# Batch 0's k loaded in fp32, its last tiles normalised in halves, v spread by VectorE: an attention and MLP kernel on one core

## The chip, the cores and the metric

The kernel runs on one core of a Trainium2 chip. The metric is the device time of one launch in microseconds. Kernels are compared by the median of several runs; three runs of the kernel before took 302.98, 303.24 and 303.75 us.

The core has a matrix engine (TensorE, PE in the profile; its weight loads are PEld), VectorE (DVE), ScalarE (ACT), GpSimd (POOL) and a queue engine (SyncE, SP). Matrix products land in PSUM, everything else lies in SBUF. DMAs are issued by SP, ScalarE or POOL and carried out by 16 DMA engines.

## The reference

Inputs are q, k and v of shape (8, 8, 576, 64): batch, heads, positions, features. The attention is linear, with ReLU features weighted by a cosine and a sine of the position, and its output goes through an MLP whose nonlinearity is h * cos(h):

```python
r = np.maximum(x, 0.0)                                   # phi, for q and for k
phi = np.concatenate([r * c, r * s], axis=-1)            # c, s: cos, sin of pi/2 * pos / 576
kv = np.einsum('bhsf,bhsd->bhfd', k_p, v)
z = np.sum(k_p, axis=2)
num = np.einsum('bhsf,bhfd->bhsd', q_p, kv)
den = np.einsum('bhsf,bhf->bhs', q_p, z)[..., None] + 1e-06
x = (num / den)                                          # to (4608, 512): token, head * 64 + feature
h = x @ w_in                                             # 512 -> 2048
out = (h * np.cos(h)) @ w_out                            # 2048 -> 512
```

## The kernel before

**Tiling.** The 576 positions of a batch lie as 96 partitions times six runs: partition p holds positions 6p to 6p + 5, and "run i" is the i-th of the six. The MLP takes the 4608 tokens in nine chunks of 512, so chunks and batches don't line up. A batch's attention output is made in five tiles of 128 tokens (the last adds 64 new ones).

**The attention of one batch.** `load` brings q, k, v from memory through POOL's queue and casts them to fp16 on the way (k16, v16, q16, two buffers each). `scaled` makes ReLU times cosine and ReLU times sine of one run, two instructions of 96x512 for all heads (96x256 for four heads, as batch 0's k is taken), on VectorE, with a few of batch 0 on ScalarE. `q_turn` turns a run of scaled q so that features lie on partitions (X): by PE and a copy out of PSUM for batches 0 and 1, by a DMA transpose on SP's queue from batch 2 on. `spread_v` copies two heads of v into rows of 66 (vz), of which the last two hold ones, so that one product gives kv and z; batch 0 does without. `kv_head` does the six matmuls of a head; ScalarE copies the result to kvz. `num_tile` makes numerator and denominator of a tile on PE (NP), and VectorE adds 1e-6 (dn), inverts (rd) and multiplies (x: the "normalise"). `x_turn` turns x to XT, the MLP's input: by PE (XP) and a copy for batches 0 and 1, by a DMA transpose from batch 2 on.

**The MLP of one chunk.** `m1_group(c, j)`, j from 0 to 15, makes 128 of the 2048 columns of h with four matmuls, then ScalarE makes the cosine (co) and VectorE the product (g). The PSUM tile of group j is free again when its g is done; there are four such tiles, two for even and two for odd j. Chunk 0's groups are done in two halves of 256 tokens, 32 half groups. `m2_part(c, m, part)` adds four of the 16 matmuls of 128 output rows; after the fourth, ScalarE copies the tile out (ost) and SP stores it.

**The order** is written out by hand: engines run their instructions in program order, and `plan` says which attention step follows which MLP step. `at(c, s, f, ...)` puts a step behind MLP step s of chunk c, in the order of the `at` calls. For chunk 0, slots 0 to 31 are its half groups (`HS` = 16), and slots z + 0 to z + 15 (z = 32) its output parts. For chunks 1 to 8, slots 0 to 15 are groups and 16 to 31 (`M2S` = 16) output parts. `plan_tiles` puts tile t of batch c + 1 at M2S + 2t, so the last one at M2S + 8; `plan_ahead` puts the scalings, turnings and copies of batch c + 2 into the same stretch.

**Buffers that matter here.** x has three buffers (`opool`): tile 3's normalise waits until tile 0's x has been turned, tile 4's until tile 1's has. co has three buffers too. The pool "att" in PSUM has two tiles, which QT, KV, NP and XP take in turn.

**The start** (lines 375 to 424): the constants CS (cosines and sines) and ID (identity for turning) through SP; k in two halves of four heads, q, v and the weights through POOL; `warm(n)`, n matmuls on zeros, which keep PE busy until the first data is there; then k's and q's scalings, the first turnings, kv, and tiles 0 to 2 of batch 0.

Of the kernel before, what the change touches and what calls it, by code (L numbers as in the profile page):

```python
# [10 lines left out]
AF = mybir.ActivationFunctionType  # L11
ALU = mybir.AluOpType
F32 = mybir.dt.float32
# [4 lines left out]
def kernel(  # L18
# [9 lines left out]
    nc = tc.nc  # L28
    B, H, S, D = q.shape
    Dm, Dff = moe_w_in.shape  # L30
    P = 128
    F = 2 * D
    R = 6
    PR = S // R
# [6 lines left out]
    RUN = R * D  # L41
# [9 lines left out]
    cs_dr = nc.inline_tensor(cs_np, name="cs_const")  # L51
# [10 lines left out]
    CS = cpool.tile([PR, 2, R], F32, name="CS")  # L62
# [13 lines left out]
    def tiles_for(b):  # L76
        st[b] = dict(
            k16=lpool.tile([PR, H * RUN], F16, name="k16", tag="k16"),
            v16=lpool.tile([PR, H * RUN + D], F16, name="v16", tag="v16"),
            q16=lpool.tile([PR, H * RUN], F16, name="q16", tag="q16"),  # L80
        )

    def load(b, which, h0=0, h1=H, i0=0, i1=R):
        src = dict(k=k, v=v, q=q)[which]
        dst = st[b][which + "16"][:, 0:H * RUN]
        dst = dst.rearrange("p (h r) -> p h r", h=H)
        nc.gpsimd.dma_start(  # L87
            out=dst[:, h0:h1, i0 * D:i1 * D],
            in_=src[b].rearrange("h (p i) d -> p h (i d)", i=R)[:, h0:h1, i0 * D:i1 * D],
        )  # L90
# [9 lines left out]
    def scaled(b, which, i, h0=0, h1=H):  # L100
        s = st[b]
        if which + "p" not in s:
            s[which + "p"] = apool.tile([PR, R, H * F], F16, name=which + "p",
                                        tag=which + "p", bufs=1)
        dst = s[which + "p"][:, i].rearrange("p (h t d) -> p h t d", t=2, d=D)
        src = s[which + "16"][:, 0:H * RUN].rearrange("p (h i d) -> p h i d", i=R, d=D)
        for t in range(2):
            if b == 0 and (which == "k" and h0 == 4 and t == 1 or which == "q" and i == 4):
                nc.scalar.activation(
                    out=dst[:, h0:h1, t, :], in_=src[:, h0:h1, i, :], func=AF.Relu,  # L110
                    scale=CS[:, t, i:i + 1],
                )
                continue
            nc.vector.tensor_scalar(  # L114
                out=dst[:, h0:h1, t, :], in0=src[:, h0:h1, i, :],
                scalar1=0.0, scalar2=CS[:, t, i:i + 1],
                op0=ALU.max, op1=ALU.mult,
            )

    def q_turn(b, i, tag="m1"):  # L120
        s = st[b]
        if i == 0:
            s["X"] = apool.tile([P, H, S], F16, name="X", tag="X")
        if b >= 2:
            nc.sync.dma_start_transpose(
                out=s["X"][:, :, i * PR:(i + 1) * PR], in_=s["qp"][:, i],
            )
            return
        if b == 1:
            if i % 2 == 0:  # L130
                s["QT"] = psA.tile([P, 2, H, P], F16, name="QT", tag="att")
            QT = s["QT"][:, i % 2]
        elif i >= 4:
            QT = psA.tile([P, 2, H, P], F16, name="QT", tag="att")[:, 0]
        else:
            QT = psM.tile([P, H, P], F16, name="QT", tag=tag)
        for h in range(H):
            nc.tensor.matmul(  # L138
                QT[:, h, 0:PR], lhsT=s["qp"][:, i, h * F:(h + 1) * F], rhs=ID[0:PR, 0:PR],
                is_transpose=True,  # L140
            )
        if b == 1 and i % 2 == 0:
            return
        i0 = i - (b == 1)
        dst = s["X"][:, :, i0 * PR:(i + 1) * PR]
        if b == 0 and i == 2:
            nc.vector.tensor_copy(out=dst, in_=QT[:, :, 0:PR])
        elif b == 1 and i > 1:
            nc.vector.tensor_copy(
                out=dst.rearrange("p h (a c) -> p a h c", a=2),  # L150
                in_=s["QT"][:, :, :, 0:PR],
            )
        elif b == 1:
            nc.scalar.activation(
                out=dst.rearrange("p h (a c) -> p a h c", a=2),
                in_=s["QT"][:, :, :, 0:PR], func=AF.Copy,
            )
        else:
            nc.scalar.activation(out=dst, in_=QT[:, :, 0:PR], func=AF.Copy)

    def spread_v(b, h):
        s = st[b]
        if h == 0:
            s["vz"] = apool.tile([PR, H, R, VS], F16, name="vz", tag="vz", bufs=1)
            nc.gpsimd.memset(s["vz"][:, :, :, D:VS], 1.0)  # L165
        src = s["v16"][:, 0:H * RUN].rearrange("p (h i d) -> p h i d", i=R, d=D)
        nc.scalar.activation(  # L167
            out=s["vz"][:, h:h + 2, :, 0:D], in_=src[:, h:h + 2], func=AF.Copy,
        )

    def kv_head(b, h):
        s = st[b]
# [24 lines left out]
                func=AF.Copy,  # L197
            )

    def num_tile(b, t):  # L200
        s = st[b]
        c0 = min(t * P, S - P)
        NP = psA.tile([P, 2, 512], F32, name="NP", tag="att")
        for h in range(H):
            o = (h % 4) * (D + 1)
            nc.tensor.matmul(  # L206
                NP[:, h // 4, o:o + D + 1],
                lhsT=s["X"][:, h, c0:c0 + P], rhs=s["kvz"][:, h],
                start=True, stop=True,
            )  # L210
        np4 = NP[:, :, 0:4 * (D + 1)].rearrange("p a (h e) -> p a h e", e=D + 1)
        dn = opool.tile([P, 2, 4, 1], F32, name="dn", tag="dn")
        nc.vector.tensor_scalar(  # L213
            out=dn, in0=np4[:, :, :, D:D + 1], scalar1=1e-6, scalar2=None, op0=ALU.add,
        )
        rd = opool.tile([P, 2, 4, 1], F32, name="rd", tag="rd")
        nc.vector.reciprocal(out=rd, in_=dn)  # L217
        x = opool.tile([P, Dm], F16, name="x", tag="x")
        nc.vector.tensor_tensor(  # L219
            out=x.rearrange("p (a h e) -> p a h e", a=2, e=D),  # L220
            in0=np4[:, :, :, 0:D], in1=rd.broadcast_to((P, 2, 4, D)), op=ALU.mult,
        )
        s["x", t] = x

    def x_turn(b, t):
        x = st[b]["x", t]
# [65 lines left out]
    def at(c, s, f, *args):  # L292
        plan.setdefault((c, s), []).append((f, args))
# [8 lines left out]

    def plan_stage0():
        at(0, 1, q_turn, 0, 4)
        at(0, 2, scaled, 0, "q", 5)
        at(0, 3, x_turn, 0, 2)
        at(0, 5, q_turn, 0, 5)
        at(0, 8, num_tile, 0, 3)
        at(0, 14, x_turn, 0, 3)
        at(0, HS + 6, num_tile, 0, 4)  # L310
        at(0, HS + 12, x_turn, 0, 4)
        z = 2 * HS
        for i in range(R):
            at(0, z + i // 2, scaled, 1, "k", i)
            at(0, z + 3 + i // 2, scaled, 1, "q", i)
        for n in range(4):
            at(0, z + 1 + n, spread_v, 1, 2 * n)
        for h in range(4):
            at(0, z + 4, kv_head, 1, h)
        for i in range(2):  # L320
            at(0, z + 5, q_turn, 1, i)
        for h in range(4, H):
            at(0, z + 5, kv_head, 1, h)
        for i in range(2, R):
            at(0, z + 5 + i // 2, q_turn, 1, i)
        for n, f, t in ((7, num_tile, 0), (8, num_tile, 1), (9, x_turn, 0),
                        (10, num_tile, 2), (10, x_turn, 1), (12, num_tile, 3),
                        (12, x_turn, 2), (13, x_turn, 3), (14, num_tile, 4),
                        (15, x_turn, 4)):
            at(0, z + n, f, 1, t)  # L330
        for i, n in enumerate((9, 10, 10, 11, 12, 13)):
            at(0, z + n, scaled, 2, "k", i)
        for n in range(4):
            at(0, z + 12 + n, spread_v, 2, 2 * n)
        for i, n in enumerate((-1, 1, 2, 4, 6, 8)):
            at(0 if n < 0 else 1, z + 15 if n < 0 else n, scaled, 2, "q", i)
            at(0 if n < 0 else 1, z + 15 if n < 0 else n, q_turn, 2, i)
        at(1, 9, loads, 3)
        for h in range(H):
            at(1, 5 + h // 4, kv_head, 2, h)  # L340
# [32 lines left out]
            f(*args)  # L373

    with tc.manual_schedule():
        nc.sync.dma_start(out=CS, in_=cs_dr.ap())
        nc.sync.dma_start(out=ID, in_=id_dr.ap())
        nc.vector.memset(WU, 0.0)
        nc.vector.memset(PIH, math.pi / 2.0)  # L379
        nc.scalar.activation(out=WS, in_=PIH, func=AF.Sin)  # L380
        tiles_for(0)
        load(0, "k", 0, 4)
        load(0, "k", 4, 8)
        load(0, "q", 0, H, 0, 4)
        load(0, "v", 0, 4)
        load(0, "v", 4, 8)
# [13 lines left out]
        def warm(n):  # L400
            for _ in range(n):
                nc.tensor.matmul(W, lhsT=WU[:, 0:P], rhs=WU, start=True, stop=True)  # L402

        warm(29)
        for h0 in (0, 4):
            for i in range(R):
                scaled(0, "k", i, h0, h0 + 4)
# [64 lines left out]
```

## Time and profile before

| what | value |
|---|---|
| median of three runs | 303.24 us |
| the profiled execution: its own time, its span | 303.31 us, 301.50 us |
| mean granted TensorE clock | 0.997 |
| start to 12.16 us | PE busy 9.82, DVE 6.27, ACT 4.52, POOL 8.41 |
| chunk 0's groups, 19.07 to 37.46 (18.39) | PE 16.66, DVE 15.08, ACT 16.29 |
| chunk 0's output and batch 1, 37.46 to 58.66 (21.20) | PE 20.30, DVE 17.46, ACT 12.02 |
| chunk 1, 58.66 to 89.12 (30.46) | PE 30.46, DVE 21.59, ACT 17.57 |
| chunk 4, 150.23 to 180.68 (30.45) | PE 30.45, DVE 21.30, ACT 17.09 |

The rows by stretch give each engine's busy time within it. A busy PE is not PE at its peak, since matmuls are pipelined and their ends are modelled. A line of a timeline reads: start, length (of all instructions merged in the line), engine, line of the kernel, operation, output and inputs, sizes, count, and in brackets the engine's idle time just before with what ended it. The costliest rows on the page (busy us, mean ns of one, idle before):

```profile
L272 PE MATMUL M<-w_out_sb,g 128*128 128x512 f16 x576 | 132.3, 379 | 0.1
L262 DVE TENSOR_TENSOR g<-M,co 128x512 f16<-128x512 f32 (+1 forms) x160 | 99.2, 635 | 51.3 <-ACT co L259 51.0
L253 PE MATMUL M<-XT,w_in_sb 128*128 128x512 f16 (+1 forms) x640 | 129.5, 358 | 1.7 <-DVE g L262 0.9
L167 ACT ACTIVATE vz<-v 96x768 f16<-96x768 f16 x28 | 21.9, 830 | 0.0
```

### The profile page before, as it was taken

How to read it: one execution, taken by the hardware profiler on the slowest of the kernel's cores; microseconds unless marked ns; L12 is line 12 of the kernel's file. 1: busy time of each engine (PE TensorE's matmuls, PEld its weight loads, DVE VectorE, ACT ScalarE, POOL GpSimd, SP SyncE). 2: the span in 40 equal slices, each digit the busy share in tenths (PEclk: the TensorE clock that was granted, in tenths of full speed). 3: DMA queues.
4: the chain of work that ended last, by engine and by line, in shares of the span. 5: the costliest groups of instructions: out<-in, count | busy, mean ns of one | idle time of the engine just before them, and what ended most of it. 6: DMA issues, size and time to landing. Idle time of an engine off the chain costs nothing.

```text
span 301.5 us, 5553 instructions
## 1 busy us (share of the span) xinstructions
PE 291.5 (97%) x2091; PEld 152.7 (51%) x2091; DVE 192.4 (64%) x482; ACT 164.5 (55%) x265; POOL 28.1 (9%) x47
## 2 busy tenths in 40 slices
PE   8898999899999999999999999999999999999993
PEld 3667766454544554455445544554455444444441
DVE  2777996788579675967396839786765257007600
ACT  2578953877157715771577158715772178127521
POOL 8432103003000200021001100000000000000000
PEclk9999999999999999999999999999999999999998
DMA  7999999997996299439973997326612510121022
GB/s 102 196 205 206 204 205 204 238 188 112 190 182 154 38 187 218 112 94 172 216 145 82 166 200 162 88 61 125 154 37 52 130 41 0 35 74 33 0 70 70
DMA packets 73483, 38.81 MB, mean 129 GB/s; under 512 B 46320, under 2 KB 68848, under 8 KB 73456
## 3 DMA queue, kind: packets, MB, share of 16 engines
q0 software_dynamic: 23856, 18.35, 40.4%
q1 hardware_dynamic: 49600, 20.10, 32.4%
q8 instruction: 16, 0.26, 0.4%
q14 instruction: 11, 0.09, 0.1%
HBM read 36.74 MB, written 9.44 MB: 153 GB/s over the span
## 4 chain that ended last, share of the span: by engine, by line
PE 88%; DVE 5%; DMA 3%; ACT 2%; issue 1%; POOL 0%; ACTq 0%; POOLq 0%
PE M L272 41%; PE M L253 38%; PE KV L180 4%; PE NP L206 3%; DMA q<-in_q_dram 3%; DVE g L262 2%; DVE x L219 1%; ACT co L259 1%; PE QT L138 1%; PE KV L190 1%; PE XP L238 1%; DVE qp L114 1%; POOL k L87 0%; DVE rd L217 0%; ACT XT L246 0%
## 5 line engine op out<-in xcount | busy, mean ns | idle before, releaser
L272 PE MATMUL M<-w_out_sb,g 128*128 128x512 f16 x576 | 132.3, 379 | 0.1
L262 DVE TENSOR_TENSOR g<-M,co 128x512 f16<-128x512 f32 (+1 forms) x160 | 99.2, 635 | 51.3 <-ACT co L259 51.0
L253 PE MATMUL M<-XT,w_in_sb 128*128 128x512 f16 (+1 forms) x640 | 129.5, 358 | 1.7 <-DVE g L262 0.9
L259 ACT ACTIVATE co<-M,PIH 128x512 f32<-128x512 f32 (+1 forms) x160 | 102.2, 645 | 28.4 <-PE M L253 26.2
L253 PEld LDWEIGHTS <-w_in_sb 128*128 128x128 f16 x640 | 61.3, 98 | 61.1 <-issue 2.6
L272 PEld LDWEIGHTS <-g 128*128 128x128 f16 x576 | 53.8, 98 | 58.7 <-issue 0.3
L279 ACT ACTIVATE ost<-M 128x512 f32<-128x512 f32 x36 | 21.5, 598 | 89.0 <-PE M L272 81.3
L219 DVE TENSOR_TENSOR x<-NP,rd 128x512 f16<-128x512 f32 x40 | 27.7, 691 | 18.8 <-DMA XT<-x 17.7
L114 DVE TENSOR_SCALAR kp<-k,CS 96x512 f16<-96x512 f16 (+1 forms) x102 | 28.6, 348 | 4.8 <-DMA k<-in_k_dram 4.8
L114 DVE TENSOR_SCALAR qp<-q,CS 96x512 f16<-96x512 f16 x94 | 28.1, 346 | 0.2 <-DMA q<-in_q_dram 0.2
L167 ACT ACTIVATE vz<-v 96x768 f16<-96x768 f16 x28 | 21.9, 830 | 0.0
L206 PEld LDWEIGHTS <-X 128*128 128x128 f16 x320 | 15.5, 98 | 8.3 <-issue 0.2
L206 PE MATMUL NP<-kvz,X 128*128 128x65 f16 x320 | 17.0, 194 | 0.0
L165 POOL MEMSET vz<- 96x96 f16 x7 | 1.3, 188 | 146.0 <-PE KV L180 118.1
L180 PEld LDWEIGHTS <-kp 96*128 96x128 f16 x336 | 12.5, 98 | 3.1
L180 PE MATMUL KV<-vz,kp 96*128 96x65 f16 x336 | 13.0, 193 | 0.0
L213 DVE TENSOR_SCALAR dn<-NP 128x8 f32<-128x8 f32 x40 | 6.5, 162 | 9.3 <-PE NP L206 8.7
L402 PE MATMUL W<-WU 128*128 128x512 f16 x35 | 10.7, 466 | 1.2 <-DVE PIH L379 1.2
L217 DVE RECIPROCAL rd<-dn 128x8 f32<-128x8 f32 x40 | 8.1, 203 | 1.4
L195 ACT ACTIVATE kvz<-KV 128x260 f16<-128x260 f32 x16 | 6.2, 387 | 4.4 <-PE KV L180 2.0
L87 POOL DMA_DIRECT2D q<-in_q_dram x9 | 7.0, 775 | 7.3 <-DVE qp L114 3.7
L87 POOL DMA_DIRECT2D k<-in_k_dram x9 | 6.9, 769 | 3.5 <-DVE g L262 2.1
(27 smaller groups left out, 58.6 us busy)
## 6 DMA issues: line engine op xcount, KB each, us to landing
out_dram<-ost SPq DMA_DIRECT2D x24, 192.0 KB, 2.4
k<-in_k_dram POOLq DMA_DIRECT2D x7, 576.0 KB, 9.5
v<-in_v_dram POOLq DMA_DIRECT2D x7, 576.0 KB, 12.9
q<-in_q_dram POOLq DMA_DIRECT2D x7, 576.0 KB, 7.4
out_dram<-ost SPq DMA_DIRECT2D x24, 128.0 KB, 2.4
w_in_sb<-in_moe_w_in_dram POOLq DMA_DIRECT2D x4, 512.0 KB, 13.9
w_out_sb<-in_moe_w_out_dram POOLq DMA_DIRECT2D x4, 512.0 KB, 19.4
out_dram<-ost SPq DMA_DIRECT2D x24, 64.0 KB, 2.0
```

The costliest lines, as they stand in the source:

```text
L87: nc.gpsimd.dma_start(out=dst[:, h0:h1, i0 * D:i1 * D], in_=src[b].rearrange("h (p i) d -> p h (i d)", i=R)[:, h0:h1, i0 * D:i1 * D],)
L114: nc.vector.tensor_scalar(out=dst[:, h0:h1, t, :], in0=src[:, h0:h1, i, :], scalar1=0.0, scalar2=CS[:, t, i:i + 1], op0=ALU.max, op1=ALU.mult,
L167: nc.scalar.activation(out=s["vz"][:, h:h + 2, :, 0:D], in_=src[:, h:h + 2], func=AF.Copy,)
L180: nc.tensor.matmul(s["KV"][:, h, 0:n], lhsT=s["kp"][:, i, h * F:(h + 1) * F], rhs=s["vz"][:, h, i, 0:n], start=(i == 0), stop=(i == R - 1),)
L206: nc.tensor.matmul(NP[:, h // 4, o:o + D + 1], lhsT=s["X"][:, h, c0:c0 + P], rhs=s["kvz"][:, h], start=True, stop=True,)
L219: nc.vector.tensor_tensor(out=x.rearrange("p (a h e) -> p a h e", a=2, e=D), in0=np4[:, :, :, 0:D], in1=rd.broadcast_to((P, 2, 4, D)), op= ...
L253: nc.tensor.matmul(M1[:, n0:n1], lhsT=w_in_sb[:, i, j * P:(j + 1) * P], rhs=XT[:, i, c * CH + n0:c * CH + n1], start=(i == 0), stop=(i == ...
L259: nc.scalar.activation(out=co[:, n0:n1], in_=M1[:, n0:n1], func=AF.Sin, bias=PIH, scale=1.0,)
L262: nc.vector.tensor_tensor(out=st["g", c][:, j, n0:n1], in0=M1[:, n0:n1], in1=co[:, n0:n1], op=ALU.mult,)
L272: nc.tensor.matmul(M2, lhsT=st["g", c][:, j, m * P:(m + 1) * P], rhs=w_out_sb[:, j], start=(j == 0), stop=(j == NJT - 1),)
L279: nc.scalar.activation(out=ost, in_=M2, func=AF.Copy)
L402: nc.tensor.matmul(W, lhsT=WU[:, 0:P], rhs=WU, start=True, stop=True)
```

## The change

Five things are altered. The two halves of batch 0's k go through SP's queue, uncast, into an fp32 tile k32, which `scaled` then reads; CS and ID go through ScalarE's queue. X of batch 0's run 2 is copied by ScalarE instead of VectorE. `spread_v` stays on ScalarE for batch 1 alone and goes to VectorE for batches 2 to 7. `num_tile` can leave out the normalise, which `normalise` then does by halves of the heads; batch 0's tiles 3 and 4 use this, one half behind each of the next two half groups. And some steps move: batch 0's last q turning from slot 5 to 6, its tile 3 from 8 to 9, the turning of tile 4 from HS + 12 to HS + 11; of batch 1 the turnings of tiles 2 and 3 by one slot, that of tile 4 from z + 15 to behind group 2 of chunk 1. Fillers at the start are 26 instead of 29.

```diff
-        src = s[which + "16"][:, 0:H * RUN].rearrange("p (h i d) -> p h i d", i=R, d=D)
+        src = s["k32" if b == 0 and which == "k" else which + "16"]
+        src = src[:, 0:H * RUN].rearrange("p (h i d) -> p h i d", i=R, d=D)
...
-        if b == 0 and i == 2:
-            nc.vector.tensor_copy(out=dst, in_=QT[:, :, 0:PR])
-        elif b == 1 and i > 1:
+        if b == 1 and i > 1:
...
-        nc.scalar.activation(
-            out=s["vz"][:, h:h + 2, :, 0:D], in_=src[:, h:h + 2], func=AF.Copy,
-        )
+        dst = s["vz"][:, h:h + 2, :, 0:D]
+        if b == 1:
+            nc.scalar.activation(out=dst, in_=src[:, h:h + 2], func=AF.Copy)
+        else:
+            nc.vector.tensor_copy(out=dst, in_=src[:, h:h + 2])
...
-    def num_tile(b, t):
+    def num_tile(b, t, whole=True):
...
+        s["x", t] = x
+        s["norm", t] = (x.rearrange("p (a h e) -> p a h e", a=2, e=D), np4, rd)
+        if whole:
+            normalise(b, t, 0, 2)
+
+    def normalise(b, t, a0, a1):
+        x4, np4, rd = st[b]["norm", t]
         nc.vector.tensor_tensor(
-            out=x.rearrange("p (a h e) -> p a h e", a=2, e=D),
-            in0=np4[:, :, :, 0:D], in1=rd.broadcast_to((P, 2, 4, D)), op=ALU.mult,
-        )
-        s["x", t] = x
+            out=x4[:, a0:a1], in0=np4[:, a0:a1, :, 0:D],
+            in1=rd[:, a0:a1].broadcast_to((P, a1 - a0, 4, D)), op=ALU.mult,
+        )
...
-        at(0, 5, q_turn, 0, 5)
-        at(0, 8, num_tile, 0, 3)
-        at(0, 14, x_turn, 0, 3)
-        at(0, HS + 6, num_tile, 0, 4)
-        at(0, HS + 12, x_turn, 0, 4)
+        at(0, 6, q_turn, 0, 5)
+        for t, n in ((3, 9), (4, HS + 6)):
+            at(0, n, num_tile, 0, t, False)
+            at(0, n + 1, normalise, 0, t, 0, 1)
+            at(0, n + 2, normalise, 0, t, 1, 2)
+            at(0, n + 5, x_turn, 0, t)
...
-                        (12, x_turn, 2), (13, x_turn, 3), (14, num_tile, 4),
-                        (15, x_turn, 4)):
+                        (13, x_turn, 2), (14, x_turn, 3), (14, num_tile, 4)):
             at(0, z + n, f, 1, t)
+        at(1, 2, x_turn, 1, 4)
...
-        nc.sync.dma_start(out=CS, in_=cs_dr.ap())
-        nc.sync.dma_start(out=ID, in_=id_dr.ap())
+        tiles_for(0)
+        st[0]["k32"] = gpool.tile([PR, H * RUN], F32, name="k32", tag="g")
+        k32_v = st[0]["k32"].rearrange("p (h r) -> p h r", h=H)
+        k0_v = k[0].rearrange("h (p i) d -> p h (i d)", i=R)
+        for h0 in (0, 4):
+            nc.sync.dma_start(out=k32_v[:, h0:h0 + 4], in_=k0_v[:, h0:h0 + 4])
+        nc.scalar.dma_start(out=CS, in_=cs_dr.ap())
+        nc.scalar.dma_start(out=ID, in_=id_dr.ap())
...
-        tiles_for(0)
-        load(0, "k", 0, 4)
-        load(0, "k", 4, 8)
...
-        warm(29)
+        warm(26)
```

## The prediction

> **What bounds the kernel now.** I read the page first, then the chain of waits, and then TensorE's and VectorE's timelines wherever that chain leaves TensorE.
>
> ```profile
> PE 291.5 (97%) x2091; PEld 152.7 (51%) x2091; DVE 192.4 (64%) x482; ACT 164.5 (55%) x265; POOL 28.1 (9%) x47
> PE 88%; DVE 5%; DMA 3%; ACT 2%; issue 1%; POOL 0%; ACTq 0%; POOLq 0%
> ```
>
> TensorE (PE) ends the program. From 58.83 us the chain names nothing but PE until the last output copy, so a saving counts only where PE stands still, and work added elsewhere costs only where it makes PE stand still. PE stands still in three places. The start (timeline of VectorE, 0 to 13):
>
> ```profile
> 6.00 4.23 DVE L114 TENSOR_SCALAR kp<-k,CS 96x256 f16<-96x256 f16 x18 [4.84 <-DMA k<-in_k_dram]
> 10.40 2.61 DVE L114 TENSOR_SCALAR qp<-q,CS 96x512 f16<-96x512 f16 x8 [0.17 <-DMA q<-in_q_dram]
> ```
>
> VectorE scales k from 6.00 to 10.23 and q from 10.40, when q has landed (the chain: q issued at 2.78, 7.60 long). PE's first turning follows at 11.07. Two limits nearly coincide: k's scaling, 0.17 us ahead, and q's landing.
>
> Chunk 0's first product, 19 to 38 (PE's timeline):
>
> ```profile
> 22.72 0.51 PE L138 MATMUL QT<-ID,qp 96*128 96x96 f16 x8 [0.30 <-DVE qp L114]
> ...
> 27.05 1.03 PE L253 MATMUL M<-XT,w_in_sb 128*128 128x256 f16 x8 [0.50 <-DVE g L262]
> ...
> 29.13 3.22 PE L253 MATMUL M<-XT,w_in_sb 128*128 128x256 f16 x28 [0.39 <-ACT XT L246]
> ...
> 34.74 1.03 PE L253 MATMUL M<-XT,w_in_sb 128*128 128x256 f16 x8 [0.39 <-DVE g L262]
> ```
>
> The brackets give PE's idle time and its releaser: q's run 5 scaled late, g delayed by a normalise, tile 3's turning late, g again.
>
> The end of batch 1 (PE, 53 to 60):
>
> ```profile
> 54.12 1.03 PE L272 MATMUL M<-w_out_sb,g 128*128 128x512 f16 x4
> 55.69 0.40 PE L238 MATMUL XP<-ID,x 128*128 128x128 f16 x4 [0.54 <-ACT vz L167]
> ...
> 57.05 1.02 PE L272 MATMUL M<-w_out_sb,g 128*128 128x512 f16 x4
> 58.43 0.40 PE L238 MATMUL XP<-ID,x 128*128 128x128 f16 x4 [0.36 <-DVE x L219]
> ```
>
> The first wait is put down to a ScalarE copy; but that turning reads x of tile 3, which VectorE finished at 55.63 (54.94 + 0.69), so the normalise is the true releaser.
>
> Last, where PE does not stop yet (VectorE, entering chunks 4 and 5, whose first matmuls start at 150.23 and 180.68):
>
> ```profile
> 149.36 0.69 DVE L219 TENSOR_TENSOR x<-NP,rd 128x512 f16<-128x512 f32 x1 [2.21 <-DMA XT<-x]
> ...
> 152.59 1.28 DVE L262 TENSOR_TENSOR g<-M,co 128x512 f16<-128x512 f32 x2
> ```
>
> ```profile
> 180.12 0.69 DVE L219 TENSOR_TENSOR x<-NP,rd 128x512 f16<-128x512 f32 x1 [1.49 <-DMA XT<-x]
> ...
> 183.36 1.28 DVE L262 TENSOR_TENSOR g<-M,co 128x512 f16<-128x512 f32 x2
> ```
>
> The last tile's normalise waits for a transpose by DMA, then ten scalings follow without a gap, then the first g of the next chunk.
>
> **The change, part by part.** Prices are sums on the profiled execution: 303.31 us, span 301.50 and 1.81 around it, 0.07 above the median of 303.24.
>
> *k of batch 0.* Two POOL issues (1.31 to 2.79) go; SP issues the halves from 0.75. No row shows so large a load there. On SP's queue CS (4.5 KB) landed 1.5 us after issue, a 192 KB store 2.3 us after in a stretch without loads (213 to 230), but 5.6 us in one with loads (103 to 118). Half of k reads 590 KB; the loads land 205 GB/s in fp16, 410 read, so 1.44 us. The quiet price is 1.5 + 1.44 = 2.9, landing at 3.7; POOL's own k took 4.69, which from 0.75 is 5.4. k now starts before any other load, so I take 4.5. VectorE's scaling reads fp32 instead of fp16. Its bounds for 256 elements: 0.195 apart on fp16 (seven from 8.79 lasted 1.44, the last 0.27 of it), 0.34 apart for g of 256 fp32 values from PSUM (four in 1.44 at 26.58). I take 0.263, near the middle, since the source is as wide as the second's and lies where the first's does. 18 x 0.263 = 4.73, and 0.6 more: the first twelve before ran 0.05 slower than the last six, while POOL was issuing DMAs. So k is scaled at 4.5 + 5.3 = 9.8. q lands earlier too, since the same bytes start about 0.9 sooner: about 9.6. q's scaling starts near 9.95 instead of 10.40: **-0.45**. Ends: -1.0 (q's landing then decides) and +1.6 (5.4 + 18 x 0.34 + 0.6 = 12.1 against 10.4).
>
> [...]
>
> CS and ID move to ScalarE's queue, two issues (0.35 and 0.42) ahead of a table load whose first user comes at 7.45: nothing, with 4 us of cover. v has to be there for PE at 12.16 and 13.5, less the gain; it stands behind 1.5 us less on POOL. Three fewer fillers, 0.22 each, end before the first turning: nothing.
>
> *X of run 2 by ScalarE.* VectorE loses 0.56 at 15.38 just ahead of tile 0's normalise, which then waits for PE's numerator (15.77): **-0.05**. ScalarE has 0.7 idle there.
>
> *Chunk 0's first product.* q's run 5 is turned one slot later; a group of 0.437 (4 x 0.109) fills PE's gap (22.26 to 22.72). g then runs to the new slot 9: numerator at 24.35, g 9 at 25.40, dn and rd 0.43, halves of 0.34 with a g of 0.34 between. Halving only spreads the delay: the second half ends at 27.6, the turning starts at 27.7 instead of 27.92, its copy at 28.1, and the second half of the chunk at 28.75 instead of 29.13. For tile 4, g is no longer late at 34.74, but x is ready 6.0 us into this half and the turning, moved a slot up, stands waiting for it from 5.5: the stall moves and stays. **-0.38** in all; ends 0 and -1.2 (both g stalls gone as well).
>
> *End of batch 1.* Tile 3's turning moves behind one more output part and tile 4's into chunk 1. From 53.64 PE then has 0.26 + 0.86 + 0.22 + 0.86 + 0.22 + 0.26 + 0.86 = 3.54 without a wait (x of tile 3 is ready at 55.63, its turning due at 55.84), so chunk 1 starts at 57.18 instead of 58.66; tile 4's 0.22 comes back later: **-1.26**. VectorE gets batch 2's four copies here and its first g is 0.5 late, under the 0.84 that PE had spare.
>
> *v of batches 3 to 7 by VectorE.* Four copies in each second product leave ScalarE, which PE does not wait for, so nothing is won. No row shows such a copy. Scalings of 256 and 512 elements from SBUF start 0.195 and 0.263 apart, so 768 gives 0.33; the other end is 0.56, a 768 copy out of PSUM. I take 0.33, as both sides lie in SBUF. They stand in slots 8 to 14, all behind the last tile's normalise, which waits for the DMA; so 1.32 us comes ahead of the next chunk's first g. The matmul group 4 needs that g's PSUM buffer, 4 x 0.863 = 3.45 after the chunk starts. Spare time before: chunk 4, 153.68 - 153.28 = 0.40, so PE stops 0.92; chunk 5, 184.13 - 184.05 = 0.08, so 1.24; chunk 2, VectorE was free at 90.63, so g ends at 92.64 against 92.57: 0.07; chunk 3 (free at 121.12) just fits; chunk 6, where VectorE was idle some 4 us, hides it. **+2.23**. With 0.56 it is 5.8.
>
> Sum: -0.45 - 0.05 - 0.38 - 1.26 + 2.23 = +0.09, so 303.31 becomes **303.4**.
>
> **Rivals.** (A) is the sum. (B) *The copies cost nothing*: the last normalise starts early enough. It started 1.89 us before chunk 3 but only 0.87 and 0.56 before 4 and 5, as loads in the same stretch held up the transposes (7.7 us to land against 2.4 without). From 1.8 us before on, the stalls vanish: 303.4 - 2.2 = 301.2. For it: the spread among three alike stretches. Against: nothing in the change moves those loads. (C) *k gains nothing*: q's packets, on POOL's queue from 2.6 on, share the engines with k's, as stores took 5.6 instead of 2.3. With k at 6.5 the start gets 1.5 worse than now: 305.3 at the worst, 304.4 with k at 5.5. Against: k is ahead of all loads. [...] (D) *Slower*: the copies run at the PSUM row's 0.56, and PE stops 5.8 us at chunks 2 to 5: 307.0; from about 0.39 a copy the total passes 0.3%. For it: the scattered rows of 64 they write; against: kp's scaling writes such rows too at 0.195 for 256.
>
> **How the numbers follow.** A 0.43, B 0.25, C 0.16, D 0.16. About 0.3% (0.9 us) is what this kernel's times can tell from no change. Faster: B and 0.08 of A's lower edge, 0.33. Same: 0.28 of A and 0.04 of C, 0.32. Slower: 0.07 of A, 0.12 of C, D: 0.35. A alone spans 302.2 to 304.6 (its two uncertain terms, start and stalls, about 0.8 each); the range reaches to B's 301.2 and to C's 305.3, leaving out most of D.
>
> **What would show it.** Right: k's scaling from about 4.5, 0.26 apart; chunk 1 starting 1.5 us nearer to the tile-3 numerator; group 4 of chunks 4 and 5 waiting about 1 us for g. Wrong: no wait of PE for g after 60 us (B), q's scaling after 10.4 (C), copies of 0.5 (D).

## The result: slower, and beyond the range of the forecast

The changed kernel takes 306.61 us (median of 22 runs, 304.14 to 308.58), the kernel before, run beside it, 303.75 (22 runs, 302.98 to 306.84). The ratio of the means is 1.0076, with a 95% interval of [1.0049, 1.0104]. The forecast was 303.4 us, its range 301.2 to 305.3; only rival D, at 307.0, named a longer time.

The profiled run of the changed kernel took 304.14 us, one of its quickest. The page of it (first lines, and the chain that ended last):

```profile
span 302.4 us, 5546 instructions
PE 291.1 (96%) x2088; PEld 152.3 (50%) x2088; DVE 197.6 (65%) x507; ACT 147.6 (49%) x242; POOL 29.3 (10%) x45
...
PE 76%; DMA 11%; DVE 9%; ACT 1%; issue 1%; DVEq 0%; ACTq 0%
PE M L260 35%; PE M L279 31%; DMA XT<-x 10%; PE KV L181 4%; DVE g L269 3%; DVE kp L115 3%; PE NP L207 3%; DMA k<-in_k_dram 2%; PE QT L139 1%; DVE qp L115 1%; ACT co L266 1%; PE KV L191 1%; DVE vz L170 1%; DVE x L227 1%; PE XP L245 1%
```

TensorE is as busy as before (291.1 us against 291.5). What is new is in the chain: TensorE's share fell from 88% to 76%, and a transpose by DMA (XT<-x, 10%) and VectorE's copies of v (vz, line 170) now stand in it. So the chain leaves TensorE in the middle of the program, where it did not before.

The start, VectorE's timeline and then TensorE's:

```profile
5.68 5.24 DVE L115 TENSOR_SCALAR kp<-k,CS 96x256 f16<-96x256 f32 x18 [4.53 <-DMA k<-in_k_dram]
10.85 2.17 DVE L115 TENSOR_SCALAR qp<-q,CS 96x512 f16<-96x512 f16 x8
```

```profile
11.50 1.04 PE L139 MATMUL QT<-ID,qp 96*128 96x96 f16 x16 [1.80 <-DVE qp L115]
12.38 2.84 PE L191 MATMUL KV<-v,kp 96*128 96x128 f16 x48
```

k arrives 0.32 us earlier than before (5.68 against 6.00), but eighteen scalings now take 5.24 instead of 4.23, and q's scaling starts at 10.85 instead of 10.40. Ahead of the first turning TensorE stands idle for 1.80 us, where it was 0.91.

Chunk 0's first product and the end of batch 1 (TensorE's timeline):

```profile
27.15 0.28 PE L245 MATMUL XP<-ID,x 128*128 128x128 f16 x2
27.71 0.28 PE L245 MATMUL XP<-ID,x 128*128 128x128 f16 x2 [0.29 <-DVE x L227]
...
28.68 3.22 PE L260 MATMUL M<-XT,w_in_sb 128*128 128x256 f16 x28 [0.25 <-DVE g L269]
...
34.17 0.28 PE L245 MATMUL XP<-ID,x 128*128 128x128 f16 x2
34.61 0.28 PE L245 MATMUL XP<-ID,x 128*128 128x128 f16 x2 [0.16 <-DVE x L227]
...
55.43 0.42 PE L207 MATMUL NP<-kvz,X 128*128 128x65 f16 x8
55.69 1.02 PE L279 MATMUL M<-w_out_sb,g 128*128 128x512 f16 x4
56.55 1.67 PE L260 MATMUL M<-XT,w_in_sb 128*128 128x512 f16 x7
```

Here the change brings what it was forecast to bring. The brackets are small (0.29, 0.25, 0.16), two of a tile's four turnings run ahead of the second half of its normalise (27.15 and 34.17), the two waits of batch 1's end are gone, and chunk 1 starts at 56.55 instead of 58.66.

The later chunks, TensorE at the start of chunk 3 and at the groups 4 of chunks 4 and 5:

```profile
118.61 1.68 PE L260 MATMUL M<-XT,w_in_sb 128*128 128x512 f16 x7 [0.76 <-DMA XT<-x]
...
153.15 4.04 PE L260 MATMUL M<-XT,w_in_sb 128*128 128x512 f16 x18 [0.46 <-DVE g L269]
...
184.53 2.75 PE L260 MATMUL M<-XT,w_in_sb 128*128 128x512 f16 x12 [0.78 <-DVE g L269]
```

Counted from matmul start to matmul start (less the pace of 0.216 us) these waits are 0.92, 0.62 and 0.94 us; the bracket is smaller, because it starts at the modelled end of the matmul before (0.379 behind its start, for a pace of 0.216). In the kernel before only chunk 3 had one, of 0.20.

From stage to stage, the two profiled runs differ so (starts of matmuls, us):

| stage | before | after | difference | forecast |
|---|---|---|---|---|
| to batch 0's first KV matmul | 12.16 | 12.38 | +0.22 | -0.45 |
| KV to chunk 0's second product | 25.30 | 24.41 | -0.89 | -0.43 |
| from there to chunk 2's start (end of batch 1, chunk 1 with tile 4's turning) | 51.66 | 50.44 | -1.22 | -1.26 |
| chunk 2, up to chunk 3's start | 30.66 | 31.38 | +0.72 | 0 |
| chunks 4 and 5 | 60.91 | 62.47 | +1.56 | +2.16 (and 0.07 in chunk 2) |
| last chunk and last output | 32.32 | 32.74 | +0.42 | 0 |
| sum, with 0.01 left in the others | | | +0.82 | +0.09 |

The +0.42 of the last chunk lies behind the last matmul, on the way of the last tile to memory: from that matmul's start to the end of the span it is 4.91 us before and 5.34 after, and 4.79 to 5.49 over the profiles of all kernels below, so it is scatter and not the change.

That explains 304.14, and not 306.61. The remaining 2.5 us are not in this profile, but the clocks of the runs point to them: of the 22 runs, the four with a mean granted clock of 0.995 or more took 304.14 to 305.57, and the eighteen with 0.985 to 0.994 took 306.03 to 308.58.

### The profile page after: what moved, and what is told of

The parts are those of the page before. It is cut to its first block, busy times and chain, and to the rows that moved or that the text cites. A ratio compares the mean times of both kernels' runs of the same rounds, so it can differ in the third digit from the quotient of the medians.

```text
span 302.4 us, 5546 instructions
## 1 busy us (share of the span) xinstructions
PE 291.1 (96%) x2088; PEld 152.3 (50%) x2088; DVE 197.6 (65%) x507; ACT 147.6 (49%) x242; POOL 29.3 (10%) x45
## 4 chain that ended last, share of the span: by engine, by line
PE 76%; DMA 11%; DVE 9%; ACT 1%; issue 1%; DVEq 0%; ACTq 0%
PE M L260 35%; PE M L279 31%; DMA XT<-x 10%; PE KV L181 4%; DVE g L269 3%; DVE kp L115 3%; PE NP L207 3%; DMA k<-in_k_dram 2%; PE QT L139 1%; DVE qp L115 1%; ACT co L266 1%; PE KV L191 1%; DVE vz L170 1%; DVE x L227 1%; PE XP L245 1%
## 5 line engine op out<-in xcount | busy, mean ns | idle before, releaser
L227 DVE TENSOR_TENSOR x<-NP,rd 128x512 f16<-128x512 f32 (+1 forms) x42 | 27.9, 665 | 19.3 <-DMA XT<-x 18.1
L115 DVE TENSOR_SCALAR kp<-k,CS 96x512 f16<-96x512 f16 (+1 forms) x102 | 30.0, 346 | 4.5 <-DMA k<-in_k_dram 4.5
L170 DVE COPY vz<-v 96x768 f16<-96x768 f16 x24 | 8.3, 348 | 0.0
L139 PE MATMUL QT<-ID,qp 96*128 96x96 f16 x96 | 5.6, 206 | 1.8 <-DVE qp L115 1.8
```

Of the source, the lines that this page charges most:

```text
L115: nc.vector.tensor_scalar(out=dst[:, h0:h1, t, :], in0=src[:, h0:h1, i, :], scalar1=0.0, scalar2=CS[:, t, i:i + 1], op0=ALU.max, op1=ALU.mult,
L139: nc.tensor.matmul(QT[:, h, 0:PR], lhsT=s["qp"][:, i, h * F:(h + 1) * F], rhs=ID[0:PR, 0:PR], is_transpose=True,)
L170: nc.vector.tensor_copy(out=dst, in_=src[:, h:h + 2])
L227: nc.vector.tensor_tensor(out=x4[:, a0:a1], in0=np4[:, a0:a1, :, 0:D], in1=rd[:, a0:a1].broadcast_to((P, a1 - a0, 4, D)), op=ALU.mult,)
```

## The experiments

All are timed beside the kernel before on the same chip (its medians were 303.39, 303.63, 303.65 and 303.73 us in the four sets). Medians in us, ten runs unless noted; "chunk 3" is TensorE's wait at that chunk's start in the one profiled run, "groups" those in chunks 4 and 5. The four sets are after_again to e3_both, b_warm33 to e6b_x5_v_act, e7_v_only to e10_early_loads, and the rest; a difference between kernels of two sets carries the scatter between sets too.

| kernel | fillers | k of batch 0 | v, batches 3-7 | us | chunk 3 | groups |
|---|---|---|---|---|---|---|
| before | 29 | POOL, fp16 | ScalarE | 303.4 to 303.7 | 0.20 | 0 |
| after | 26 | SyncE, fp32 | VectorE | 306.61 (22 runs) | 0.92 | 0.62, 0.94 |
| after_again | 26 | SyncE | VectorE | 306.40 (4) | 1.06 | 0.76, 0.75 |
| e1_warm33 | 33 | SyncE | VectorE | 305.08 | 0.93 | 0.64, 1.08 |
| e2_v_act | 26 | SyncE | ScalarE | 305.85 | 1.97 | 0 |
| e3_both | 33 | SyncE | ScalarE | 303.19 | 1.23 | 0, 0.22 |
| b_warm33 | 33 | POOL | ScalarE | 303.39 | 0.38 | 0, 0.08 |
| e4_k_pool_v_act | 33 | POOL | ScalarE | 301.79 | 0.75 | 0.12, 0 |
| e6a_x5 | 33 | SyncE | VectorE | 302.72 | 1.09 | 0, 0 |
| e6b_x5_v_act | 33 | SyncE | ScalarE | 302.97 | 1.15 | 0, 0 |
| e7_v_only | 33 | POOL | VectorE | 305.55 | 0.29 | 0.69, 1.21 |
| e8_k_only | 33 | SyncE | ScalarE | 305.21 | 0.96 | 0, 0 |
| e9_k_pool_x5 | 33 | POOL | VectorE | 301.37 (5) | 0.15 | 0, 0 |
| e10_early_loads | 33 | POOL | VectorE | 301.44 (6) | 0 | 0, 0 |
| e11_k_v_pieces | 33 | SyncE | ScalarE | 304.72 | 1.30 | 0, 0 |
| e12_k_early | 33 | SyncE | ScalarE | 303.85 | 0 | 0, 0 |
| e13_all_x5_early | 33 | SyncE | VectorE | 302.05 | 0 | 0, 0 |

b_warm33, e7, e8, e11 and e12 are made from the kernel before, the others from the changed one, with its slot moves, halved normalises and X's run 2 on ScalarE.

**The changed kernel again, and with 33 fillers.** The first has no edit. The second:

```
-        warm(26)
+        warm(33)
```

> The changed kernel once more, beside the others on one chip. Stall theory (VectorE's copies in front of the next chunk's first g): about 304 in every run, since the profiled execution was 304.14. Clock theory (TensorE idle from 9.70 to 11.50 us before the first turning, so that its clock is sometimes halved afterwards): a wide spread up to 308, the long runs with a mean granted clock of 0.985 to 0.993 instead of 0.997, and a profile of a long run shows half clock in the first 30 us.

> The changed kernel with 33 fillers instead of 26, which end at about 11.2 us, just ahead of the first turning at 11.50. Clock theory: all runs near 304, clock 0.997. Stall theory, or a clock that drops at the chunk boundaries: no different from the changed kernel, 304 to 308.

306.40 and 305.08 us. The profile of the repetition caught what the first profile had not. TensorE's timeline, and stretches of 3.41 us, as long as the clock was halved in this profile, laid off from the rise of the clock at 5.02 (from, to; width; busy time and instructions of PE, PEld, DVE, ACT, POOL; granted clock; DMA share; GB/s):

```profile
11.75 1.41 PE L139 MATMUL QT<-ID,qp 96*128 96x96 f16 x16 [2.89 <-DVE qp L115]
12.96 3.95 PE L191 MATMUL KV<-v,kp 96*128 96x128 f16 x48
```

```profile
5.02:8.43 3.41, 3.41 (x17) 1.57 (x16) 2.54 (x8) 0.17 (x1) 2.36 (x4) 1.00 1.26 224
8.43:11.85 3.42, 0.53 (x5) 0.10 (x4) 3.42 (x14) 2.33 (x6) 1.80 (x1) 1.00 1.33 203
11.85:15.26 3.41, 3.41 (x38) 3.41 (x38) 1.42 (x6) 1.51 (x2) 3.26 (x3) 0.50 1.39 198
15.26:18.67 3.41, 3.40 (x64) 2.95 (x62) 0.90 (x3) 2.12 (x4) 1.55 (x2) 1.00 1.28 206
```

The granted clock is 0.50 from 11.85 to 15.26. The 48 matmuls of KV, 2.84 us long in the first profile, take 3.95, and the first group of the first product starts at 20.93 instead of 19.25. In the 3.42 us just ahead of the halving TensorE was busy for 0.53. In the first profile the clock had risen later, at 6.72 instead of 5.02; the same stretches, laid off from there:

```profile
6.72:10.13 3.41, 2.98 (x14) 1.18 (x12) 3.41 (x14) 1.84 (x5) 0.80 (x2) 1.00 1.36 204
10.13:13.55 3.42, 2.04 (x37) 1.90 (x38) 2.89 (x12) 2.17 (x4) 3.42 (x2) 1.00 1.28 205
```

Here the clock stayed at 1.00 behind a stretch in which TensorE was busy for 2.04 of 3.42 us. The instant at which the clock rises changes from profile to profile, also for one kernel: 6.72 in the first profile and 5.02 in the repetition, 6.36 in the kernel before, 4.27 in e3_both. It also decides when the fillers end: in the first profile they start 0.43 us apart before it and 0.216 after it. A clock that rises early ends 26 fillers early, at 8.7 in the repetition against 9.5 in the first profile, and lengthens the idle time to the first turning, which starts when its data is ready: 1.80 us by the bracket in the first profile, 2.89 in the repetition (3.06 if the last filler, which started at 8.48, is taken to end 0.216 later). The halving followed the longer of the two; whether the length of the gap decides, or TensorE's busy share of such a stretch, no run separates.

**v back on ScalarE, and both edits together.** The edit of e2_v_act, to which e3_both adds the 33 fillers:

```
-        if b == 1:
+        if b != 2:
             nc.scalar.activation(out=dst, in_=src[:, h:h + 2], func=AF.Copy)
```

> The changed kernel with v of batches 3 to 7 spread by ScalarE as before, batch 2 by VectorE. Stall theory: the 2.2 us at chunks 2 to 5 go, so 304.1 becomes about 301.9, and if the clock drops because of these stalls, the spread goes too. Clock theory with its place at the start: 2.2 us less, but the same spread of 4 us and the same low clocks.

> Both: v of batches 3 to 7 by ScalarE and 33 fillers. If stalls and start add up: about 301.9 in every run, clock 0.997. If the start has no part in it: the same as with v by ScalarE alone.

305.85 and 303.19 us. In the profile of e2_v_act the clock was halved for 6.82 us, 11.42 to 18.24, and the first product began 3.1 us later than in the first profile of the changed kernel (22.39 against 19.25); all ten runs had a mean clock of 0.984 to 0.994. With 33 fillers none went below 0.996. So the fillers are worth 1.3 to 1.5 us with the copies on VectorE (305.08 against 306.40 and 306.61) and 2.7 without (303.19 against 305.85), and the copies 1.9 with 33 fillers (305.08 against 303.19). Both lose time, but the two losses don't simply add: with 26 fillers the copies cost only 0.55 (306.40 against 305.85). The profile of e2_v_act has 3.41 us of half clock more than that of after_again and a longer wait at chunk 3 (1.97 against 1.06); why is not shown. With both mended the time is that of the kernel before.

**More fillers in the kernel before.**

```
-        warm(29)
+        warm(33)
```

> The kernel before with 33 filler matmuls ahead of the first turning in place of 29 (four more, about 0.85 us, which fills the 0.91 us in which TensorE stands idle there). If it is an idle TensorE ahead of the first turning that lets the clock be halved, the runs of 304.9 to 305.5 us with a mean clock of 0.992, which the kernel before shows here and there, are gone: every run has a clock of 0.996 or more, the median is 303.0 to 303.4 and the spread under 0.8 us. If those runs come from something else, some still lie near 305 with a clock of 0.992. If the fillers themselves cost, the median rises by up to 0.3.

303.39 us, 302.75 to 304.05, no clock below 0.997. The kernel before has the same weakness, only less: 25 of its 103 runs in the four sets had a mean clock of 0.994 or less, and took 304.88 to 307.96 us; with 26 fillers 32 of 36 runs had; with 33, in all the kernels of the table, none of 121. The four fillers more cost nothing that can be measured.

**k of batch 0 through POOL again, v on ScalarE.** From e3_both:

```
-        for h0 in (0, 4):
-            nc.sync.dma_start(out=k32_v[:, h0:h0 + 4], in_=k0_v[:, h0:h0 + 4])
-        nc.scalar.dma_start(out=CS, in_=cs_dr.ap())
-        nc.scalar.dma_start(out=ID, in_=id_dr.ap())
+        nc.sync.dma_start(out=CS, in_=cs_dr.ap())
+        nc.sync.dma_start(out=ID, in_=id_dr.ap())
...
+        load(0, "k", 0, 4)
+        load(0, "k", 4, 8)
```

> The changed kernel with 33 fillers, v of batches 2 to 7 on ScalarE, and k of batch 0 loaded again by POOL into fp16 (CS and ID on SyncE's queue), so that of the change only the slot moves, the halved normalises of batch 0 and X's run 2 on ScalarE are left. Theory 1, loading k in fp32 costs at the start (first half of k 4.83 us on the way, q's scaling from 10.85 instead of 10.40): the first turning falls back from 11.52 to about 11.07, all that follows is 0.2 to 0.4 earlier, 302.8 to 303.0. Theory 2, the order of POOL's loads is also what makes chunk 3 begin late (its wait of 0.9 to 1.2 us on the turned rows of batch 3, against 0.20 in the kernel before): that wait falls back to 0.2 as well and the time is 301.8 to 302.2. Rival, the fp32 loads cost nothing: 303.2 as with k by SyncE.

301.79 us (301.35 to 302.15), ratio to the kernel before 0.9917 [0.9887, 0.9947]. The first turning is at 10.97, as theory 1 has it; the time is that of theory 2, though chunk 3's wait is 0.75 and not 0.2. Neither is exact, but k's part costs 1.40 us (303.19 less 301.79, of two sets; within this set, e6b_x5_v_act of the next experiment less this one, 1.18), where a gain had been forecast. And what is left of the change, the slot moves, the halved normalises and X's run 2 on ScalarE, brings 1.60 against b_warm33.

**Five buffers for x.**

```
-        x = opool.tile([P, Dm], F16, name="x", tag="x")
+        x = opool.tile([P, Dm], F16, name="x", tag="x", bufs=5)
```

> The changed kernel with 33 fillers and five buffers for the normalised rows x, so that no normalise waits until the DMA transpose of a tile before has read its buffer. Theory 1, the late groups of chunks 4 and 5 (TensorE waits of 0.64 and 1.08 us) come from VectorE's copies of v standing behind a normalise that waits for its buffer: with five buffers the normalise does not wait, both waits vanish, and 305.1 falls to 303.2 to 303.6. Rival, the copies' own time on VectorE (4 x 0.27 us) delays the group whatever they stand behind: 304.7 to 305.1. Chunk 3's wait (0.93) can shrink as well if the turned rows are late because SyncE's queue stands behind the blocked normalise: then 302.4 to 302.8.

> As the run before, and v of batches 2 to 7 on ScalarE. With v off VectorE the groups of chunks 4 and 5 do not wait, so five buffers can only act on chunk 3's wait (1.23 us in the run with three buffers). If the turned rows are late because SyncE's queue is held by a normalise that waits for its buffer, the wait falls to 0.2 to 0.6 and the time from 303.2 to 302.2 to 302.8; if they are late because the loads of batch 5 landed late, nothing changes: 303.0 to 303.4.

302.72 and 302.97 us: with five buffers, VectorE's copies cost nothing (302.72 is not above 302.97), with three they cost 1.89. It is not the copies' duration alone that hurt, but their place behind a normalise that waits. VectorE's timeline of the changed kernel, entering chunk 5, whose first matmul starts at 180.13:

```profile
179.50 0.69 DVE L227 TENSOR_TENSOR x<-NP,rd 128x512 f16<-128x512 f32 x1 [2.37 <-DMA XT<-x]
180.10 0.35 DVE L170 COPY vz<-v 96x768 f16<-96x768 f16 x1
180.37 0.61 DVE L115 TENSOR_SCALAR qp<-q,CS 96x512 f16<-96x512 f16 x2
...
183.53 0.35 DVE L170 COPY vz<-v 96x768 f16<-96x768 f16 x1
183.80 1.28 DVE L269 TENSOR_TENSOR g<-M,co 128x512 f16<-128x512 f32 x2
```

and with five buffers, before chunk 5's start at 180.62:

```profile
177.53 0.35 DVE L170 COPY vz<-v 96x768 f16<-96x768 f16 x1
177.80 0.61 DVE L115 TENSOR_SCALAR kp<-k,CS 96x512 f16<-96x512 f16 x2
178.32 0.35 DVE L170 COPY vz<-v 96x768 f16<-96x768 f16 x1
182.50 1.45 DVE L269 TENSOR_TENSOR g<-M,co 128x512 f16<-128x512 f32 x2 [3.83 <-ACT co L266]
```

In the first, a wait of 2.37 us for a transpose by DMA holds back everything behind it, and the first g of the chunk starts at 183.80, 3.7 us after the chunk's first matmul. In the second, VectorE is done at 178.7, stands idle for 3.83 us, and the first g starts 1.9 us after the chunk's first matmul. (Chunk 5 itself began 0.93 late in that run, on a transpose of X; at 303.68 us it was the slowest of the ten.) Chunk 3's wait stayed at 1.09 and 1.15, so it has another cause. (302.72 also lies below the 303.2 to 303.6 that the two waits alone would give: the profiled run of e1_warm33, from which they were read, was 0.6 quicker than its median.)

**One part alone, on the kernel before with 33 fillers.** In e7_v_only:

```
-        nc.scalar.activation(
-            out=s["vz"][:, h:h + 2, :, 0:D], in_=src[:, h:h + 2], func=AF.Copy,
-        )
+        dst = s["vz"][:, h:h + 2, :, 0:D]
+        if b == 1:
+            nc.scalar.activation(out=dst, in_=src[:, h:h + 2], func=AF.Copy)
+        else:
+            nc.vector.tensor_copy(out=dst, in_=src[:, h:h + 2])
```

In e8_k_only the part of the change that loads k of batch 0 in fp32 through SyncE's queue and moves CS and ID to ScalarE's.

> The kernel before with 33 fillers (303.39 us), and of the change only VectorE's copies of v for batches 2 to 7. Theory, copies behind a blocked normalise make one group late in chunk 4 and one in chunk 5: TensorE waits there of 0.6 and 0.9 to 1.1, sum 1.5 to 1.7, 304.9 to 305.2. My prediction's own sum for these copies, 2.23: 305.6. Rival, the copies lost time only together with the other edits: 303.4.

> The kernel before with 33 fillers (303.39 us), and of the change only k of batch 0 in fp32 through SyncE's queue. By my prediction's working k lands earlier and all begins 0.45 earlier, and the moved POOL loads bring nothing: 302.9 to 303.0. Theory after the runs so far: the scalings and q's load set a start that is 0.3 to 0.5 later, and POOL issues the loads of batch 5 0.5 later in chunk 2 (a gap of 0.86 in place of 0.36 ahead of its q load), so that chunk 3 waits 0.5 to 0.9 longer: 304.0 to 304.6. Rival, either is only the scatter of single profiles: 303.4.

305.55 us: v alone costs 2.16, the 2.23 of the forecast. 305.21 us: k alone costs 1.82, more than expected for this run, where the forecast had a gain of 0.45. The profiles show less of it than the medians: the profiled run of e8_k_only was the quickest of its ten (304.59), that of b_warm33 nearly its slowest (304.02), and they lie 0.57 apart, about as much as their waits at chunk 3 (0.96 against 0.38). This wait begins on POOL, ahead of batch 5's loads. POOL's timeline in the kernel before and then in e8_k_only:

```profile
103.06 0.19 POOL L165 MEMSET vz<- 96x96 f16 x1 [30.35 <-PE KV L180]
103.61 0.77 POOL L87 DMA_DIRECT2D q<-in_q_dram  x1 [0.36 <-DVE g L262]
```

```profile
103.28 0.18 POOL L166 MEMSET vz<- 96x96 f16 x1 [30.37 <-PE KV L181]
104.33 0.78 POOL L87 DMA_DIRECT2D q<-in_q_dram  x1 [0.86 <-DVE g L263]
```

Between the same two instructions 0.36 us became 0.86. In all nine profiles with k on SyncE's queue and these loads in their old place it is 0.80 to 0.90, in the five with k through POOL 0.31 to 0.36.

**The best mix, and earlier loads.** e9_k_pool_x5 is the changed kernel with k through POOL, 33 fillers and five buffers, each as above. e10_early_loads adds:

```
-        if 1 < c and c + 2 < B:
+        if c == 2:
             at(c, 1, loads, c + 2)
+        if 1 < c and c + 3 < B:
+            at(c, M2S + 7, loads, c + 3, "kqv")
```

> The changed kernel with 33 fillers, k of batch 0 through POOL in fp16, v of batches 2 to 7 by VectorE, and five buffers for the rows x. If v on VectorE costs time only through a normalise that waits for its buffer, it costs nothing here: 301.3 to 301.8, no group of chunks 4 and 5 late, and chunk 3's wait stays at about 0.7. If the copies cost by themselves, 302.3 or more.

> As the run before, and the loads of batches 5 to 7 are put ahead of the VZ memset of the batch before them on POOL, with k first, so that POOL issues them when k's buffer comes free in the first product of the chunk, some 4 to 6 us earlier. Theory: the DMA transposes of a second product land only behind the landing of that v (0.34 to 0.46 us behind it in chunks 2 to 4 of every run), and this makes chunk 3's first group late; with v landed early, the transposes land earlier, chunk 3's wait falls from about 0.7 to 0 to 0.2 and the time by 0.5 to 0.7 to 300.8 to 301.1. Rival, the transposes are slow by themselves or wait for something else: nothing changes, or the loads collide with the output stores of the chunk before and with the turning of x: 301.5 or more.

301.37 us (five runs, 301.09 to 301.96), ratio to the kernel before 0.9921 [0.989, 0.995], and 301.44. The first is in the expected range, though chunk 3's wait is 0.15 where 0.7 was expected; its chain is TensorE 88%, as in the kernel before. The second misses: chunk 3's wait is gone, but it was only 0.15 in the first, so there was nothing to win.

**Is it the loads that make k dear?** e11_k_v_pieces (from e8_k_only) gives POOL its old number of loads; e12_k_early and e13_all_x5_early are e8_k_only and e6a_x5 with the earlier loads of e10.

```
-        load(0, "v", 0, 4)
-        load(0, "v", 4, 8)
+        for h0 in range(0, 8, 2):
+            load(0, "v", h0, h0 + 2)
```

> The kernel before with 33 fillers and k of batch 0 in fp32 through SyncE's queue (305.21 us), and v of batch 0 loaded by POOL in four pieces of two heads in place of two of four, so that POOL issues as many loads as in the kernel before. Theory, POOL's gap of 0.86 us ahead of the q load of batch 5 hangs on how many loads went before it: the gap is 0.36 again, chunk 3's wait falls from 0.96 to 0.2 to 0.4, and the time to 304.2 to 304.6. Rival, the gap comes from k's being on SyncE's queue: gap 0.86, wait about 1, 305.0 to 305.4.

> The kernel before with 33 fillers and k of batch 0 in fp32 through SyncE's queue (305.21 us), and the loads of batches 5 to 7 ahead of the VZ memset on POOL, so that v of batch 5 lands long before the turned rows of batch 3 are due. Theory, nearly all that k costs goes through the landing of these loads: chunk 3's wait is 0, 303.6 to 304.2. Rival, the start itself is later by 0.5 or more: 304.5 or more.

> The whole change with 33 fillers and five buffers for the rows x (302.72 us), and the loads of batches 5 to 7 ahead of the VZ memset on POOL. Theory as above: chunk 3's wait of 1.09 goes, and with it 1.0 to 1.2 us: 301.5 to 301.8, no more than 0.3 above the kernel with k through POOL (301.4). Rival, k in fp32 costs at the start too: 302.2 or more.

304.72, 303.85 and 302.05 us. The number of loads is not the reason: POOL's gap is 0.90, chunk 3's wait 1.30. e11 is 0.49 below e8 all the same, on another chip, and no profile says why. Why POOL is late there stays open, and so does whether k on SyncE's queue does it or CS and ID on ScalarE's: they moved together in every run. But the way from there to TensorE is shown. Here is SyncE's queue in e8_k_only: tile 2's XT, for whose rows chunk 3's first matmul waits, and the X transpose ahead of it. Below it are the same two in e12_k_early, and POOL's first load of batch 5 there:

```profile
113.66 3.15 SPq L126 DMA_TRANSPOSE X<-qp  x1
116.90 1.22 SPq L231 DMA_TRANSPOSE XT<-x  x1
```

```profile
112.38 1.26 SPq L126 DMA_TRANSPOSE X<-qp  x1
113.74 1.21 SPq L231 DMA_TRANSPOSE XT<-x  x1
```

```profile
97.44 0.78 POOL L87 DMA_DIRECT2D k<-in_k_dram  x1 [24.54 <-DVE g L263]
```

With batch 5's loads issued from 97.44 instead of 104.33, the X<-qp transpose takes 1.26 us to issue instead of 3.15, tile 2's XT follows 3.2 us earlier, and chunk 3 starts without a wait. How much of k's loss goes this way is less sure: the time falls by 1.36 of the 1.82 against e8_k_only, by 0.87 against e11_k_v_pieces of the same set, and in the changed kernel by 0.67 (e6a_x5 to e13_all_x5_early); with k through POOL the same early loads win nothing (e10). Counted from the start of chunk 2's second product, in e8_k_only v of batch 5 lands at 13.53 us, the first X transpose at 13.73, then an XT and an X, and tile 2's XT at 16.02, 0.04 before chunk 3's first matmul; in the kernel before v landed at 12.42, X at 12.88 and tile 2's XT at 15.26. What is left, 0.46 of the 1.82 and the 0.6 of e13 over e10, would fit a later start, but single profiles scatter too much to show it: batch 0's first KV matmul was at 12.33 to 12.64 (mean 12.41) in the nine with k on SyncE's queue and an undisturbed clock, and at 11.62 to 12.63 (mean 12.25) in the six with k through POOL.

## Why the prediction was wrong, step by step

- **"Three fewer fillers ... end before the first turning: nothing."** This step failed. It took the fillers for work that may end early at no cost, where they also kept the clock up here (0.995 or more in all 121 runs with 33 of them, 0.994 or less in 32 of 36 with 26). And its cover was counted in one profile, in which the clock had risen late (at 6.36 us, against 5.02 in after_again and 4.27 in e3_both). Measured: 1.3 to 1.5 us (e1_warm33), 2.7 with v on ScalarE (e3_both).
- **k of batch 0, -0.45.** Wrong in size and sign, and the largest miss: +1.82 alone, +1.40 in the changed kernel. At the start the failed term is the landing: taken at 4.5, 3.75 us after the issue, it was 5.58, 4.83 after. The scalings, 0.263 apart and 5.3 long in all, were right (5.24), and so was q's landing (9.7 for 9.6); q's scaling then started at 10.85, behind the 10.4 that the prediction names as a sign of being wrong. (Its own terms end at 9.8; no row gives the further 0.15 up to its 9.95.) The landing is the condition of the rival "k gains nothing", which puts 304.4 on a landing at 5.5; the profiled run had 304.14, but through other waits, as its first KV matmul came only 0.22 later than before. Half of the loss or more (0.67 of 1.35 between e6a_x5 and e9_k_pool_x5, 1.36 of 1.82 for k alone) went by a way that the prediction did not name: taking k from POOL was costed for the start alone, and POOL's later work was taken to stay as it was. It did not; why POOL is late there stays open.
- **v by VectorE, +2.23.** Right in mechanism and place, and in size with some luck: 2.16 alone, 1.89 in the changed kernel; groups 4 of chunks 4 and 5 wait, chunk 3's does not. A copy is 0.27 apart where 0.33 was taken; with 0.27 the prediction's sum gives 0.68 and 1.00 for chunks 4 and 5 instead of 0.92 and 1.24, and the four profiles had 0.62 to 0.76 and 0.75 to 1.21. So the waits explain 1.5 to 1.9 us, and the rest of the 2.16 is in no profile. The rival of copies at 0.56 falls.
- **X's run 2, chunk 0's first product, the end of batch 1: -0.05, -0.38, -1.26.** Right in direction: -1.60 together (e4 against b_warm33) for -1.69, which is near by some luck. From the first KV matmul to chunk 2's start the two profiles differ by 2.10 (74.85 us against 76.95), and chunk 3's longer wait (0.75 against 0.38) gives part of it back. Batch 1's end is as forecast, 1.22 in the changed kernel's profile; in chunk 0, 0.89 was had for 0.43, since two of a tile's four turnings already run between the halves of its normalise, where the forecast put all four behind both, and tile 4's stall shrank to 0.16 where it was forecast to stay.

In sum, from e4_k_pool_v_act: 301.79, k +1.40, v +1.89, 26 fillers +1.53: 306.61. This adds by construction, since each part is the difference of two neighbouring medians; of the 3.2 between forecast and result, k is 1.85 (+1.40 for -0.45), the fillers 1.53, and v takes 0.34 off. The parts do not quite add from the other end: b_warm33 with +2.16, +1.82 and -1.60 gives 305.77 for the 305.08 of e1_warm33. The forecast had +0.09 from terms of both signs; a term for the fillers and one for POOL's later loads were missing.

## What to carry to other kernels

Fillers are a matter of time and not of a count: the clock rose at 4.27 us in one profile here and at 6.72 in another, and a filler took 0.43 us before and 0.216 after, so count them for the earliest rise, and see in several runs' clocks, not in one profile, whether they suffice. An instruction of VectorE that waited 2.37 us for a buffer made everything queued behind it late here; before moving work behind such an instruction, give it its buffer, and then the work may cost nothing (1.89 us with three buffers, none with five). Taking loads off a queue can shift that queue a hundred microseconds later (here by 0.5 us, for a reason that stays open): look up which chunk starts with the least slack on it (here 0.20 us of wait already) and price the shift there.

## What the runs showed of the hardware

At the start, half clock lasted 3.41 us in after_again (11.85 to 15.26) and 6.82 in e2_v_act (11.42 to 18.24), and began 6.83 us after the rise in both. In the stretch of 3.41 or 3.42 us just ahead of it TensorE was busy for 0.53 us in after_again and for 0.64 in e2_v_act; in after, e9_k_pool_x5, e3_both, b_warm33 and e12_k_early it was 2.04 to 2.32 us in the same stretch, and full clock followed. At half clock, a stretch busy for 3.05 of 3.41 us (11.42 to 14.83 of e2_v_act) was followed by another at half, and one busy throughout (11.85 to 15.26 of after_again) by full clock.

SyncE's transposes by DMA landed late while loads that POOL had started were still landing: in e12_k_early, with the loads landed early, tile 2's XT lands 11.54 us after the start of the second product, in e8_k_only, where the last of these loads lands at 13.53, at 16.02.
